# A planned attention and mixing kernel: batch 0's q without its zeros, one pair of scores a unit earlier, last stores in halves

## The chip, the core and the metric

The kernel runs on one core of a Trainium2 chip. The time is the device time of one execution in microseconds (us). The kernel before takes 584.44 us, the median of 3 runs (584.28 to 584.83). The core has a matrix engine (TensorE: PE in the profile, with its weight loads as PEld), a vector engine (VectorE: DVE), a scalar engine (ScalarE: ACT), GpSimd (POOL), and SyncE (SP), whose queue issues every DMA here. Each engine executes its own instructions in a fixed order; semaphores make one engine wait for another. The trace shows the profiled execution, one more run, of 583.05 us.

## The reference, cut to what matters

There are 8 batches, 8 heads, 576 positions and head size 64. The first four heads see a window of the last 32 positions, the other four a window of 128 positions of which every fourth counts.

```python
scores = (1.0 / np.sqrt(D)) * np.matmul(q, k.transpose(0, 1, 3, 2))
scores = np.where(masks[None, :, :, :], scores, -1000000000.0)
scores = scores - np.max(scores, axis=-1, keepdims=True)
attn = np.exp(scores)
attn = attn / (np.sum(attn, axis=-1, keepdims=True) + 1e-09)
x = np.matmul(attn, v)                      # heads side by side: (8, 576, 512)
theta = x @ w_theta
zr, zi = x * np.cos(theta), x * np.sin(theta)
y = np.einsum('ts,bsd->btd', w_tok_r, zr) + np.einsum('ts,bsd->btd', w_tok_i, zi)
u = x + y
out = u + np.maximum(u @ w_ch, 0.0)
```

## The kernel before, in words

**Attention by pairs.** A batch's 8 heads are 4 pairs; each pair takes 128 partitions, one head in the lower 64 and the other in the upper 64. On the host, q is laid out block-diagonally: `qT` holds, for each block of 32 queries, 32 columns for the first head and 32 for the second, and where one head has its values the other has zeros. So one matmul with 128 rows gives the scores of both heads against their window of 64 keys (L468), and half of the bytes of q are zeros: 576 KB per pair, of which 288 KB are values. The four pairs of batch 0 have their own places for q (`q0_0` to `q0_3`, in buffers that later stage weights).

Batch 0's mask is added on PE by matmuls with `idb` (L424). Then DVE takes the row maximum (`mx`, L430) and subtracts it (`P`, L433) in two halves of 5 and 4 blocks, ACT takes the exponential (L493), DVE sums it (`sm`, L495) and makes the reciprocal (L507, L508), POOL multiplies (L510), PE turns the result over (`pT`, L561), DVE and ACT bring it back (`pt`, L536, L539), PE multiplies by v (`o`, L617), and ACT copies the attention output out (`x`, L581). In later batches DVE adds the mask and takes the maximum in one instruction per block (L409), ACT's exponential (L504) works block by block, and DVE turns P over by 32x32 transposes (`pt`, L525).

**Weights.** The three weight matrices arrive as 64-bit integers that hold the reference's doubles' bits. `unpack` makes floats with extra bits of them in place, with steps on DVE (L332, L337, L342) and ACT (L334, L340); `split` then makes a high and a low part (ACT L350, POOL L352). `st_wth` is the staging of `w_theta` (4 pieces), `st_wtk` of the token matrix (5 early pieces for the first half of the positions, 5 late ones for the second), `st_wch` of the channel matrix (4 pieces).

**Mixing.** For each of five position tiles, theta is x times `w_theta` (L667 for batch 0, L685 later), and the trig chain makes sine and cosine of it (ACT L787, DVE L789, ACT L796, L698, L705), multiplies by x (DVE L750 or L748) and splits the result (`zh`, `zl`: ACT L644 or DVE L641, POOL L646). Then come 16 units of PE work per batch: 8 token units (4 channel blocks for each half of the positions, 27 matmuls each, L850, added to x by DVE L825 and split again into `u` by ACT L828 and POOL L830) and 8 channel units (12 matmuls each, L880, finished by DVE L859).

**What sets the order.** Batch 0 and the attention, theta and trig of batch 1 are written by a planner (`Order`). Each task is a generator that names an engine and an assumed duration, or an event that it needs; a task has a rank; whenever an engine comes free in the planner's own clock, the ready task of the lowest rank takes it. The order found is pinned. An assumed DMA takes its bytes at a fixed rate, so the order of the first part of the program depends on how many bytes the planner sees ahead of each weight. From batch 1 on, `phase(b, b + 1)` writes the 16 units of batch b with the attention and theta of batch b+1 between them; `S_AT`, `PV_AT`, `TURN_AT` say at which unit a pair's scores, value product and turning are written. Numbers 2 and 3 there are the last two pairs of batch b+1, and 4 and 5 the first two pairs of batch b+2. PE keeps that order; the other engines are ordered by a scheduler.

**The end.** After the second half of an output block is done, `finish` stores the block of 128 x 576 values (L865).

Of the kernel before, what the change touches and what calls it, by code (L numbers as in the profile page):

```python
# [8 lines left out]
F32 = mybir.dt.float32  # L9
F32R = mybir.dt.float32r  # L10
BF16 = mybir.dt.bfloat16
# [6 lines left out]
B, H, S, D = 8, 8, 576, 64  # L18
DM = H * D
NP = H // 2  # L20
QB = 32
BW = 2 * QB
NJ = S // (2 * QB)
# [20 lines left out]

S_AT = {2: 0, 3: 1, 4: 4, 5: 6}
PV_AT = {0: 0, 1: 1, 2: 2, 3: 4}
TURN_AT = {2: 0, 3: 1, 4: 5}
TURN_TH = {5: 1}  # L50
# [11 lines left out]
class Order:  # L62
# [13 lines left out]
    def pin(self, ins):  # L76
        if self.live:
            self.tc.keep_in_program_order(ins)

    def signal(self, event):  # L80
        self.events[event] = self.now

    def go(self, gen, rank=None):
        if not self.live:
            for _ in gen:
                pass
            return
        self.serial += 1
        t = [self.rank if rank is None else rank, self.serial, self.now, gen, None, 0.0]
        self.tasks.append(t)  # L90
        self.advance(t)
# [39 lines left out]
def dve(n):  # L131
    return 67 + 1.04 * n
# [6 lines left out]
def act(n):  # L139
    return 95 + 0.83 * n  # L140


def pool(n):
    return 2.36 * n


def dma(n):
    return 128 * 4 * n / 360.0


@with_exitstack
def build(ctx, tc, qT, kT, vw, wth, wtk, wch, maskb, ident, identb, outT):
    nc = tc.nc
    cp = ctx.enter_context(tc.tile_pool(name="const", bufs=1))
    ap = ctx.enter_context(tc.tile_pool(name="attn", bufs=2))
# [12 lines left out]
    pin, go, signal = od.pin, od.go, od.signal  # L168
# [20 lines left out]
    def take(tag, bufs, n=None):  # L189
        n = reserve(tag) if n is None else n  # L190
        if od.live:
            if n >= bufs:
                yield None, ("free", tag, n - bufs)
            if n:
                yield None, ("got", tag, n - 1)
            signal(("got", tag, n))
        return n

    def give(tag, n):
        if od.live:  # L200
            signal(("free", tag, n))
# [9 lines left out]
    qks, vs = {}, {}  # L211
# [15 lines left out]
    def load_va(n):  # L227
        if n >= B * NP:
            return
        b, pr = divmod(n, NP)  # L230
        r = yield from take("va", 2)
        va = ap.tile([128, VA, 128], F32, tag="va", name=f"va{b}_{pr}")
        yield "DMA", dma(VA * 128)
        pin(nc.sync.dma_start(va, vw[b, pr, :, :VA]))
        vs["a", b, pr] = (va, r)
        signal(("va", b, pr))

    def load_vb(n):
        if n >= B * NP:
            return  # L240
        b, pr = divmod(n, NP)
        if n == NP - 1:
            r = None
            vb = hp.tile([128, DM], F32R, tag="zl8", name="first_vb").bitcast(F32)
            vb = vb.rearrange("p (a b) -> p a b", b=128)
        else:
            r = yield from take("vb", 1)
            vb = ap.tile([128, NJ - VA, 128], F32, tag="vb", name=f"vb{b}_{pr}", bufs=1)
        yield "DMA", dma((NJ - VA) * 128)
        pin(nc.sync.dma_start(vb, vw[b, pr, :, VA:]))  # L250
        vs["b", b, pr] = (vb, r)
        signal(("vb", b, pr))
# [12 lines left out]
    mskb = cp.tile([128, 6, BW], BF16, name="mskb")  # L265
    idb = cp.tile([128, 128], BF16, name="idb")
    halfpi = cp.tile([128, 1], F32, name="halfpi")
    pqs, pts = [], []

    def first_loads():  # L270
        yield "DMA", dma(3 * BW + 64)
        pin(nc.sync.dma_start(mskb, maskb.bitcast(BF16)))
        pin(nc.sync.dma_start(idb, identb.bitcast(BF16)))
        for pr in range(NP):
            yield from take(f"xh{pr}", 1, 0)
            yield from take(f"u{pr}", 1, 0)
            pqs.append(hp.tile([128, 2, S], F32R, tag=f"xh{pr}", name=f"P0_{pr}").bitcast(F32)[:, 0])
            q = hp.tile([128, 2, S], F32R, tag=f"u{pr}", name=f"q0_{pr}").bitcast(F32)
            q = q.rearrange("p a b -> p (a b)").rearrange("p (a b) -> p a b", b=2 * QB)
            k = first_k[:, KE * pr:KE * pr + KE]  # L280
            yield "DMA", dma(2 * S)
            pin(nc.sync.dma_start(q, qT[0, pr]))
            yield "DMA", dma(KE)
            pin(nc.sync.dma_start(k, kT[0, pr]))
            qks[0, pr] = (q, k, None)
            if pr == 0:
                yield "DMA", dma(128)
                pin(nc.sync.dma_start(idt, ident))
            signal(("qk", 0, pr))
        for pr in range(NP // 2):  # L290
            v = first_v[:, NJ * 128 * pr:NJ * 128 * pr + NJ * 128].rearrange("p (a b) -> p a b", b=128)
            yield "DMA", dma(NJ * 128)
            pin(nc.sync.dma_start(v, vw[0, pr]))
            for h, t in (("a", v[:, :VA]), ("b", v[:, VA:])):
                vs[h, 0, pr] = (t, None)
                signal(("v" + h, 0, pr))
        for pr in range(NP // 2, NP):
            yield from load_va(pr)
            yield from load_vb(pr)
# [555 lines left out]
    def finish(b, e, g, ps, rel):  # L855
        ts = slice(HS * g, HS * g + HS)
        x = xf[b, e]
        yield "DVE", dve(HS)
        pin(nc.vector.scalar_tensor_tensor(out=x[:, ts], in0=ps, scalar=0.0, in1=x[:, ts],  # L859
                                           op0=ALU.max, op1=ALU.add))  # L860
        give(*rel)
        signal(("out", b, e, g))
        if g == 1:
            yield "DMA", dma(S)
            pin(nc.sync.dma_start(outT[b, e], x))  # L865

# [20 lines left out]
    def phase(b, nb):  # L887
# [5 lines left out]
        while n <= TH_AT:  # L893
            for p in S_AT:
                if S_AT[p] == n and nb + p // NP < B:
                    go(scores(nb + p // NP, p % NP))
# [56 lines left out]
    UH = {d: reserve(f"u{d}") for d in range(NC)}  # L953
    od.live = True
    go(first_loads(), 0)
    go(consts(), 0)
    for p in range(NP):
# [29 lines left out]
        phase(b, b + 1)  # L987


_INS = ["qT", "kT", "vw", "wth", "wtk", "wch", "maskb", "ident", "identb"]  # L990


def _arrays(inp):
    import numpy as np
    q, k, v = inp["q"], inp["k"], inp["v"]

    def perm(a):
        a = np.array(a, dtype=a.dtype)
        dil = a[:, H // 2:].reshape(B, H // 2, S // 4, 4, D).transpose(0, 1, 3, 2, 4)
        a[:, H // 2:] = dil.reshape(B, H // 2, S, D)  # L1000
        return a

    q, k, v = perm(q), perm(k), perm(v)
    qT = np.zeros((B, NP, 2, D, 2 * NJ, 2, QB), q.dtype)
    qh = q.reshape(B, NP, 2, 2 * NJ, QB, D).transpose(0, 1, 2, 5, 3, 4)
    for hh in range(2):
        qT[:, :, hh, :, :, hh] = qh[:, :, hh]
    qT = qT.reshape(B, NP, 128, 2 * NJ, 2 * QB)
    kT = np.zeros((B, NP, 128, S + 32), k.dtype)
    kT[..., 32:] = k.transpose(0, 1, 3, 2).reshape(B, NP, 128, S)  # L1010
    vp = np.zeros((B, H, S + 32, D), v.dtype)
    vp[:, :, 32:] = v
    vp = vp.reshape(B, NP, 2, S + 32, D).transpose(0, 1, 3, 2, 4).reshape(B, NP, S + 32, 128)
    vw = np.stack([np.concatenate([vp[:, :, BW * j + QB * e:BW * j + QB * e + BW] for e in range(2)], axis=2)
                   for j in range(NJ)], axis=3)
    wth = inp["moe_w_theta"].reshape(NC, 128, DM).transpose(1, 0, 2)
    wch = inp["moe_w_ch"].reshape(NC, 128, DM).transpose(1, 0, 2)
    wr, wi = inp["moe_w_tok_r"].T, inp["moe_w_tok_i"].T
    wtk = np.stack([wr[128 * c:128 * c + 128] for c in range(4)] +
                   [wi[128 * c:128 * c + 128] for c in range(4)] +  # L1020
                   [np.concatenate([wr[512:], wi[512:]], axis=0)], axis=1)
    m = np.zeros((6, 4, QB, BW), bool)
    for n, (j, bound) in enumerate(((1, 0), (0, 0), (2, 144), (4, 288), (6, 432), (7, 432))):
        for quad in range(4):
            qb = 2 * j + quad // 2
            p = QB * qb + np.arange(QB)[:, None]
            c = QB * qb - QB + np.arange(BW)[None, :]
            m[n, quad] = (p - c >= 0) & (p - c < 32) & (c >= 0) & ((p >= bound) == (c >= bound))

    maskb = np.where(m.transpose(1, 2, 0, 3).reshape(128, 6, BW), 0, 0xD000).astype(np.uint16)  # L1030
    wth, wtk, wch = (np.ascontiguousarray(w).view(np.int64) for w in (wth, wtk, wch))
    ident = np.eye(128, dtype=np.float32)
    identb = np.where(ident > 0, 0x3F80, 0).astype(np.uint16)
    return dict(qT=qT, kT=kT, vw=vw, wth=wth, wtk=wtk, wch=wch, maskb=maskb, ident=ident, identb=identb)


# [20 lines left out]
```

## Time and profile before

| | us |
|---|---|
| median of 3 runs | 584.44 |
| the profiled execution | 583.05 |
| its span, first to last instruction | 581.3 |
| PE busy in the span | 553.6 (95%) |
| DVE busy | 378.0 (65%) |
| ACT busy | 344.3 (59%) |
| POOL busy | 222.6 (38%) |
| first matmul of scores | at 6.8 |
| early token unit's last input of batch 0 done | at 66.4 |
| start of batch 1's token units | at 143.8 |
| last instruction of the last output on DVE | 577.9 to 578.3 |

The part of the profile that counts here is in three stages: a start in which PE has little to do (to about 66 us), a long middle in which PE is nearly always busy, and a tail after the last matmul. The prediction shows the lines of each.

### The profile page before, as it was taken

How to read it: one execution, taken by the hardware profiler on the slowest of the kernel's cores; microseconds unless marked ns; L12 is line 12 of the kernel's file. 1: busy time of each engine (PE TensorE's matmuls, PEld its weight loads, DVE VectorE, ACT ScalarE, POOL GpSimd, SP SyncE). 2: the span in 40 equal slices, each digit the busy share in tenths (PEclk: the TensorE clock that was granted, in tenths of full speed). 3: DMA queues.
4: the chain of work that ended last, by engine and by line, in shares of the span. 5: the costliest groups of instructions: out<-in, count | busy, mean ns of one | idle time of the engine just before them, and what ended most of it. 6: DMA issues, size and time to landing. Idle time of an engine off the chain costs nothing.

```text
span 581.3 us, 13989 instructions
## 1 busy us (share of the span) xinstructions
PE 553.6 (95%) x5464; PEld 502.7 (86%) x5464; DVE 378.0 (65%) x1156; ACT 344.3 (59%) x939; POOL 222.6 (38%) x206
## 2 busy tenths in 40 slices
PE   5997898999999999999999999999999999999997
PEld 4743787989999899989999899988999899989997
DVE  3879798865666668756765768766775767545112
ACT  1498967767553884459554784349555685266110
POOL 2228855625133352316224262225323263326120
PEclk9999699899999999999999999999999999999999
DMA  8991437502648054551747145560746223321002
GB/s 298 399 367 42 145 110 259 192 0 87 204 144 220 6 191 146 162 162 49 240 146 179 47 151 180 139 191 4 252 143 172 90 83 101 71 94 62 22 0 82
DMA packets 45010, 81.91 MB, mean 141 GB/s; under 512 B 3856, under 2 KB 17936, under 8 KB 44944
## 3 DMA queue, kind: packets, MB, share of 16 engines
q1 hardware_dynamic: 44944, 81.02, 43.6%
q8 instruction: 43, 0.70, 0.5%
q14 instruction: 23, 0.19, 0.1%
HBM read 64.49 MB, written 16.52 MB: 139 GB/s over the span
## 4 chain that ended last, share of the span: by engine, by line
DVE 32%; PE 29%; ACT 26%; POOL 6%; issue 4%; DMA 2%; SPq 1%; ACTq 0%; DVEq 0%; POOLq 0%
DVE pt L525 14%; PE y L850 13%; ACT P L504 10%; PE c L880 7%; PE th L685 4%; DVE P L409 4%; POOL zl L646 3%; DVE xh L599 2%; POOL P L510 2%; ACT zh L644 2%; PE s L468 2%; ACT K L698 2%; ACT K L787 2%; ACT cos L705 2%; ACT th L796 2%
## 5 line engine op out<-in xcount | busy, mean ns | idle before, releaser
L830 POOL TENSOR_TENSOR u<-x,u 128x288 fp32r<-128x288 f32 x64 | 54.8, 857 | 189.2 <-ACT u L828 189.2
L525 DVE STREAM_TRANSPOSE pt<-P 32x288 f32<-32x288 f32 x224 | 104.9, 468 | 12.5 <-POOL P L510 8.9
L880 PE MATMUL c<-u,late_wc 128*128 128x288 f32 x768 | 108.9, 295 | 0.0
L880 PEld LDWEIGHTS c<-u,late_wc 128*128 128x128 f32 x768 | 105.9, 188 | 2.8
L850 PE MATMUL y<-wtkh,zh 128*128 128x288 f32 x288 | 90.1, 313 | 1.1 <-ACT zh L644 1.1
L850 PE MATMUL y<-wtkh,zl 128*128 128x288 f32 x288 | 86.2, 299 | 4.0 <-POOL zl L646 4.0
L828 ACT CAST u<-x 128x288 fp32r<-128x288 f32 x64 | 27.4, 430 | 104.0 <-DVE x L825 104.0
L646 POOL TENSOR_TENSOR zl<-g,zh 128x512 fp32r<-128x512 f32 x40 | 52.6, 1317 | 94.8 <-ACT zh L644 81.9
L850 PE MATMUL y<-wtkl,zh 128*128 128x288 f32 x288 | 86.0, 298 | 0.0
L685 PE MATMUL th<-wthh,xh 128*128 128x512 f32 x224 | 75.0, 396 | 5.4 <-DVE g L748 5.2
L504 ACT ACTIVATE P<-P,mx 128x64 f32<-128x64 f32 x216 | 72.1, 335 | 13.1 <-DVE mx L498 12.4
L850 PE MATMUL y<-late_wt_b,zh 128*128 128x288 f32 x320 | 68.1, 297 | 0.0
L825 DVE TENSOR_TENSOR x<-y,x 128x288 f32<-128x288 f32 x64 | 28.6, 448 | 54.4 <-PE y L850 54.2
L850 PEld LDWEIGHTS y<-wtkh,zl 128*128 128x128 f32 x288 | 55.1, 191 | 4.7 <-POOL zl L646 4.7
L850 PEld LDWEIGHTS y<-wtkh,zh 128*128 128x128 f32 x288 | 55.0, 191 | 4.8 <-ACT zh L644 2.3
L850 PE MATMUL y<-late_wt_a,zh 128*128 128x288 f32 x256 | 57.4, 305 | 0.0
L850 PEld LDWEIGHTS y<-wtkl,zh 128*128 128x128 f32 x288 | 55.1, 191 | 0.3 <-issue 0.3
L685 PEld LDWEIGHTS th<-wthh,xh 128*128 128x128 f32 x224 | 42.0, 188 | 15.2 <-PE c L880 4.8
L510 POOL TENSOR_TENSOR P<-P,sm 128x576 f32<-128x576 f32 x32 | 37.5, 1173 | 40.7 <-DVE sm L508 17.7
L850 PEld LDWEIGHTS y<-late_wt_b,zh 128*128 128x128 f32 x320 | 51.4, 189 | 0.3
L850 PE MATMUL y<-late_wt_b,zl 128*128 128x288 f32 x160 | 47.3, 296 | 0.0
L581 ACT COPY x<-o 128x576 f32<-128x576 f32 x32 | 29.6, 924 | 28.7 <-PE o L617 23.9
(108 smaller groups left out, 1106.1 us busy)
## 6 DMA issues: line engine op xcount, KB each, us to landing
q<-in_qT_dram SPq DMA_DIRECT2D x32, 576.0 KB, 5.0
va<-in_vw_dram SPq DMA_DIRECT2D x30, 320.0 KB, 3.2
out_dram<-x SPq DMA_DIRECT2D x32, 288.0 KB, 2.1
k<-in_kT_dram SPq DMA_DIRECT2D x28, 304.0 KB, 5.2
vb<-in_vw_dram SPq DMA_DIRECT2D x29, 256.0 KB, 3.7
xd<-xq SPq DMA_DIRECT2D x24, 288.0 KB, 4.8
xn<-xd SPq DMA_DIRECT2D x24, 256.0 KB, 4.9
st_wtk<-in_wtk_dram SPq DMA_DIRECT2D x8, 576.0 KB, 8.8
```

Source lines behind the costliest of these rows:

```text
L409: pin(nc.vector.tensor_tensor_reduce(out=P[:, n], in0=ps[:, n - g0], in1=mskb[:, mask_of(pr, n)], op0=ALU.add, op1=ALU.max, scale=1.0, sca ...
L504: table(nc.scalar.activation(P[:, n], P[:, n], AF.Exp, bias=mx[:, n:n + 1], scale=SCALE, accum_out=sm[:, n:n + 1]))
L510: pin(nc.gpsimd.tensor_tensor(P, P, sm.unsqueeze(2).to_broadcast([128, NJ, BW]), op=ALU.mult))
L525: pin(nc.vector.transpose(pmats[b, pr][k0:k0 + QB, :, hh, QB * e:QB * e + QB], P[p0:p0 + QB, :, QB * o:QB * o + QB]))
L581: pin(nc.scalar.copy(dst, src))
L646: pin(nc.gpsimd.tensor_tensor(lo, z, hi.bitcast(F32), op=ALU.subtract))
L685: pe(nc.tensor.matmul(pt, l, r, start=(n == 0), stop=(n == 3 * NC - 1)))
L825: pin(nc.vector.tensor_tensor(x[:, ts], ps, x[:, ts], op=ALU.add))
L828: pin(nc.scalar.copy(uh[b, d][:, ts], x[:, ts]))
L830: pin(nc.gpsimd.tensor_tensor(ul[b, d][:, ts], x[:, ts], uh[b, d][:, ts].bitcast(F32), op=ALU.subtract))
L850: pe(nc.tensor.matmul(ps, l[:, cs], r, start=(n == 0), stop=(n == 3 * NK - 1)))
L880: pe(nc.tensor.matmul(ps, l[:, cs], r[:, ts], start=(n == 0), stop=(n == 3 * NC - 1)))
```

## The change: what it does

Three edits.

- Batch 0's q is loaded without the zeros. A new input `q0` holds the 288 KB of values per pair; they land in `q_raw` (the buffer of a tile that batch 2 uses first). `q_zero` writes the zeros of each half with two VectorE memsets per pair (64 partitions x 576 elements each), and `q_place` copies the values to their places: the lower half on ScalarE, the upper half on VectorE for pair 0 and on GpSimd for pairs 1 to 3. `mskb` and `idb` are issued behind the first q. The planner sees the new tasks, and half of q's bytes.
- `S_AT` gives the scores of pair "4" (the first pair of batch b+2) with token unit 3 in place of 4, in the five phases that have such a pair.
- The last batch's outputs are stored as two halves of 128 x 288, each as soon as it is done.

```diff
-S_AT = {2: 0, 3: 1, 4: 4, 5: 6}
+S_AT = {2: 0, 3: 1, 4: 3, 5: 6}
...
+    q_raw = cp.tile([128, 5 * DM], F32, tag="xn", name="q_raw")[:, :NP * S]
+    q_raw = q_raw.rearrange("p (n a b) -> p n a b", n=NP, b=QB)
+
+    def q_zero(pr, q, hh):
+
+        yield "DVE", 670
+        pin(nc.vector.memset(q[64 * hh:64 * hh + 64, :, QB - QB * hh:2 * QB - QB * hh], 0.0))
+        signal(("qz", pr, hh))
+
+    def q_place(pr, q, hh):
+        to, src = q[64 * hh:64 * hh + 64, :, QB * hh:QB * hh + QB], q_raw[64 * hh:64 * hh + 64, pr]
+        if hh == 0:
+            yield "ACT", act(S)
+            pin(nc.scalar.copy(to, src))
+        elif pr == 0:
+            yield "DVE", dve(S)
+            pin(nc.vector.tensor_copy(to, src))
+        else:
+            yield "POOL", pool(S)
+            pin(nc.gpsimd.tensor_copy(to, src))
+        signal(("qp", pr, hh))
+
+    def q_ready(pr, q, k):
+        for hh in range(2):
+            yield None, ("qz", pr, hh)
+            yield None, ("qp", pr, hh)
+        yield None, ("k0", pr)
+        qks[0, pr] = (q, k, None)
+        signal(("qk", 0, pr))
+
     def first_loads():
-        yield "DMA", dma(3 * BW + 64)
-        pin(nc.sync.dma_start(mskb, maskb.bitcast(BF16)))
-        pin(nc.sync.dma_start(idb, identb.bitcast(BF16)))
         for pr in range(NP):
...
-            yield "DMA", dma(2 * S)
-            pin(nc.sync.dma_start(q, qT[0, pr]))
+            for hh in range(2):
+                go(q_zero(pr, q, hh), -1)
+            yield "DMA", dma(S)
+            pin(nc.sync.dma_start(q_raw[:, pr], q0[pr]))
+            for hh in range(2):
+                go(q_place(pr, q, hh), 0)
+            if pr == 0:
+                yield "DMA", dma(3 * BW + 64)
+                pin(nc.sync.dma_start(mskb, maskb.bitcast(BF16)))
+                pin(nc.sync.dma_start(idb, identb.bitcast(BF16)))
...
-        if g == 1:
+        if b == B - 1:
+            pin(nc.sync.dma_start(outT[b, e][:, ts], x[:, ts]))
+        elif g == 1:
             yield "DMA", dma(S)
             pin(nc.sync.dma_start(outT[b, e], x))
...
+    q0 = np.ascontiguousarray(qh[0].reshape(NP, 128, 2 * NJ, QB))
```

The planner gives the first part of the program another order on every engine. Three places of it follow; lines behind the new functions stand 35 or more higher in the changed kernel (L430 is L465 there).

DVE, the start of the program, before (`mx`, `P` and `sm` are row maximum, scores and sum; `s_1_0` is pair 1's first half of scores):

```order
L303 MEMSET halfpi 128x1
L430 TENSOR_REDUCE mx_0_116<-s_0_0_118 128x5
L433 TENSOR_TENSOR P_0_104<-s_0_0_118,mx_0_116 128x320
L430 TENSOR_REDUCE mx_0_116<-s_0_5_135 128x4
L433 TENSOR_TENSOR P_0_104<-s_0_5_135,mx_0_116 128x256
L430 TENSOR_REDUCE mx_1_147<-s_1_0_151 128x5
L495 TENSOR_REDUCE sm_0_117<-P_0_104 128x9
L433 TENSOR_TENSOR P_1_114<-s_1_0_151,mx_1_147 128x320
```

And in the change:

```order
L276 MEMSET q_0_98 64x18x32 x2
L338 MEMSET halfpi 128x1
L286 COPY q_0_98<-q_raw 64x18x32
L276 MEMSET q_1_117 64x18x32 x2
L465 TENSOR_REDUCE mx_0_121<-s_0_0_123 128x5
L276 MEMSET q_2_127 64x18x32 x2
L468 TENSOR_TENSOR P_0_97<-s_0_0_123,mx_0_121 128x320
L276 MEMSET q_3_146 64x18x32 x2
L465 TENSOR_REDUCE mx_0_121<-s_0_5_142 128x4
L465 TENSOR_REDUCE mx_1_159<-s_1_0_169 128x5
L468 TENSOR_TENSOR P_0_97<-s_0_5_142,mx_0_121 128x256
L468 TENSOR_TENSOR P_1_116<-s_1_0_169,mx_1_159 128x320
```

Four memsets now stand between the steps of pair 0's first softmax, and the second half of pair 0 stands behind pair 1's first maximum.

DVE again, around the scores of pair 3 in batch 0, before (`st_wth` is the staging of the theta weights):

```order
L430 TENSOR_REDUCE mx_3_226<-s_3_5_302 128x4
L433 TENSOR_TENSOR P_3_154<-s_3_5_302,mx_3_226 128x256
L332 TENSOR_SCALAR st_wth_96<-st_wth_96 128x512
L495 TENSOR_REDUCE sm_3_227<-P_3_154 128x9
L536 COPY pt_107<-pT_2_0_355 64x10x32
L536 COPY pt_107<-pT_2_5_389 64x8x32
L337 TENSOR_SCALAR st_wth_96<-st_wth_96 128x512
L507 TENSOR_SCALAR sm_3_227<-sm_3_227 128x9
```

And in the change:

```order
L465 TENSOR_REDUCE mx_3_250<-s_3_5_326 128x4
L468 TENSOR_TENSOR P_3_145<-s_3_5_326,mx_3_250 128x256
L367 TENSOR_SCALAR st_wth_101<-st_wth_101 128x512
L571 COPY pt_112<-pT_2_0_378 64x10x32
L377 SCALAR_TENSOR_TENSOR st_wth_100<-st_wth_100 128x512
L571 COPY pt_112<-pT_2_5_415 64x8x32
L372 TENSOR_SCALAR st_wth_101<-st_wth_101 128x512
L367 TENSOR_SCALAR st_wth_102<-st_wth_102 128x512
L377 SCALAR_TENSOR_TENSOR st_wth_101<-st_wth_101 128x512
L530 TENSOR_REDUCE sm_3_251<-P_3_145 128x9
L367 TENSOR_SCALAR st_wtk_0_161<-st_wtk_0_161 128x576
L377 SCALAR_TENSOR_TENSOR st_wth_102<-st_wth_102 128x512
```

Where one step of the first theta piece stood between pair 3's subtraction and its sum, there now stand seven rows, five of them steps of theta pieces 1 to 3; the first theta piece is done before pair 3's maximum.

DVE in phase 1, around the first masked maximum of pair "4" (`P_0_2099` before, `P_0_2084` in the change); `pt_109` before and `pt_114` in the change is pair 3's turned P, and each L409 row (L444 in the change) is followed by one that reads its maximum. Before:

```order
L729 STREAM_TRANSPOSE xq_1884<-x_2_2037 128x18x32
L525 STREAM_TRANSPOSE pt_109<-P_3_1886 32x9x32 x8
L597 TENSOR_TENSOR xh_2_2062<-x_2_2037,xh_2_2062 128x64
L599 TENSOR_TENSOR xh_2_2062<-x_2_2037,xh_2_2062 128x512
L825 TENSOR_TENSOR x_3_1340<-y_3_0_2067,x_3_1340 128x288
L409 ISA P_0_2099,mx_0_2100<-s_0_0_2102,mskb 128x64
L409 ISA mx_0_2100 128x1
```

And in the change:

```order
L764 STREAM_TRANSPOSE xq_1901<-x_2_2054 128x18x32
L444 ISA P_0_2084,mx_0_2085<-s_0_0_2087,mskb 128x64
L444 ISA mx_0_2085 128x1
L560 STREAM_TRANSPOSE pt_114<-P_3_1903 32x9x32 x8
L632 TENSOR_TENSOR xh_2_2079<-x_2_2054,xh_2_2079 128x64
L634 TENSOR_TENSOR xh_2_2079<-x_2_2054,xh_2_2079 128x512
L444 ISA P_0_2084,mx_0_2085<-s_0_0_2087,mskb 128x64
L444 ISA mx_0_2085 128x1
```

One of the nine masked maxima moves ahead of the eight transposes; the other eight stay behind L599, and L825 of `y_3_0` moves from ahead of them to behind them, still ahead of the step (L498) that hands the maxima to ACT.

More of the change, by code (lines that the diff above doesn't have):

```diff
@@ L151, in build @@
 @with_exitstack
-def build(ctx, tc, qT, kT, vw, wth, wtk, wch, maskb, ident, identb, outT):
+def build(ctx, tc, qT, q0, kT, vw, wth, wtk, wch, maskb, ident, identb, outT):
     nc = tc.nc
@@ L280, in first_loads @@
             k = first_k[:, KE * pr:KE * pr + KE]
-            yield "DMA", dma(2 * S)
-            pin(nc.sync.dma_start(q, qT[0, pr]))
+            for hh in range(2):
[8 more added lines that the diff above has]
+                pin(nc.sync.dma_start(idb, identb.bitcast(BF16)))
             yield "DMA", dma(KE)
             pin(nc.sync.dma_start(k, kT[0, pr]))
-            qks[0, pr] = (q, k, None)
+            go(q_ready(pr, q, k), 0)
             if pr == 0:
@@ L288, in first_loads @@
                 pin(nc.sync.dma_start(idt, ident))
-            signal(("qk", 0, pr))
+            signal(("k0", pr))
         for pr in range(NP // 2):
@@ L987, in build @@
         phase(b, b + 1)
-_INS = ["qT", "kT", "vw", "wth", "wtk", "wch", "maskb", "ident", "identb"]
+_INS = ["qT", "q0", "kT", "vw", "wth", "wtk", "wch", "maskb", "ident", "identb"]
 def _arrays(inp):
@@ L1033, in _arrays @@
     identb = np.where(ident > 0, 0x3F80, 0).astype(np.uint16)
-    return dict(qT=qT, kT=kT, vw=vw, wth=wth, wtk=wtk, wch=wch, maskb=maskb, ident=ident, identb=identb)
+    return dict(qT=qT, q0=q0, kT=kT, vw=vw, wth=wth, wtk=wtk, wch=wch, maskb=maskb, ident=ident, identb=identb)
 def kernel(**inputs):
```

## The prediction, as put on record

> **What bounds the kernel now.** I read the busy table by stages first, then the waits of PE, then the chain and the timeline at the places that the change touches. The table gives, for each stretch in us, the length and the busy us of each engine (PE, PEld, DVE, ACT, POOL), the granted clock, the share of time in which the DMA engines were busy, and what they moved.
>
> ```profile
> 6.80:30.00 23.20, 21.45 (x420) 17.27 (x422) 16.81 (x40) 8.93 (x16) 4.87 (x4) 1.00 1.03 395
> 30.00:66.40 36.40, 29.76 (x194) 16.22 (x188) 32.77 (x83) 33.05 (x68) 22.53 (x17) 0.91 0.58 211
> 66.40:76.00 9.60, 9.53 (x70) 9.30 (x72) 7.08 (x17) 9.38 (x32) 8.99 (x8) 0.82 0.00 0
> 76.00:106.00 30.00, 27.00 (x371) 23.91 (x367) 25.79 (x61) 20.13 (x76) 13.74 (x14) 0.94 0.67 221
> 106.00:143.80 37.80, 36.62 (x292) 32.94 (x288) 26.58 (x57) 28.66 (x60) 19.06 (x17) 1.00 0.18 65
> 210.00:276.00 66.00, 64.99 (x654) 60.64 (x654) 45.10 (x158) 40.65 (x121) 24.09 (x24) 1.00 0.47 144
> ```
>
> From 30 to 66.4 DVE and ACT are busy for 32.8 and 33.1 of 36.4 us: that stage ends when they have got through their work. From 6.8 to 30 DVE is busy for only 16.8 of 23.2 us, 6.4 us idle. From 66.4 on PE is the bound; in a whole batch (210 to 276) it idles 1.0 us of 66. So a us won before 66.4 is a us at the end, unless a wait behind it eats it.
>
> ```profile
> PE th L685 <- DVE g L748: 5.2, 5, 1.2
> PE s L424 <- ACT P L485: 3.0, 2, 2.0
> PE s L468 <- DMA first_k<-in_kT_dram: 3.2, 1, 3.2
> 64.85 1.58 POOL zl L646
> 66.47 8.67 PE y L850 x52
> ```
>
> The waits of PE (total, times, longest) and two pieces of the chain: the one regular wait of the batches is 5.2 us in five places, theta behind the trig chain; and the start ends where the last `zl` lets the token units run.
>
> **The loads.** In the timeline the four first issues, in the chain the piece that PE waits for, then the bandwidth in three stretches:
>
> ```profile
> 0.74 0.38 SPq L272 DMA_DIRECT2D mskb<-in_maskb_dram  x1
> 1.64 0.42 SPq L282 DMA_DIRECT2D q<-in_qT_dram  x1
> 2.11 0.43 SPq L284 DMA_DIRECT2D first_k<-in_kT_dram  x1
> 2.11 4.56 DMA first_k<-in_kT_dram
> 3.00:4.00 1.00, 0.45 (x2) 0.13 (x2) 0.00 (x0) 0.00 (x0) 0.00 (x0) 1.00 0.66 194
> 5.00:6.00 1.00, 0.00 (x0) 0.00 (x0) 0.00 (x0) 0.00 (x0) 0.00 (x0) 1.00 1.07 345
> 36.00:40.00 4.00, 4.00 (x12) 1.69 (x13) 3.05 (x6) 3.98 (x7) 2.32 (x2) 1.00 1.06 396
> ```
>
> k of pair 0 lands at 2.11 + 4.56 = 6.67, as the fourth issue behind 96 + 32 + 576 KB. In the change it is the fourth again, behind 288 + 96 + 32 KB: 288 KB less, 0.85 us at 345 GB/s. The large transfer is now issued at 0.74 in place of 1.64, so the engines no longer run at 194 GB/s on small ones until 4; I add 0.35 for that. Scores begin **1.2 us earlier** (0.7 by bytes alone at 400 GB/s; 1.8 if k lands as soon as the fixed part of a small load allows), at 5.6.
>
> The copies lie beside that:
>
> ```profile
> 20.33 0.64 ACT L581 COPY x<-o 128x576 f32<-128x576 f32 x1
> 13.34 1.15 POOL L510 TENSOR_TENSOR P<-P,sm 128x576 f32<-128x576 f32 x1 [10.56 <-DVE sm L508]
> 10.48 0.68 ACT L493 ACTIVATE P<-P 128x576 f32<-128x576 f32 x1 [8.47 <-DVE P L433]
> ```
>
> The first q lands at about 4 (issued at 0.74, a small load's 2.0 us and 0.85 us of bytes, with room), ACT's copy takes 0.64, DVE's no more: done at 4.8, ahead of k. POOL's three copies take 0.6 to 1.5 each; it has nothing to do before 13.3, and q of pair 3, behind some 2250 KB, lands near 10, ahead of ACT's first exponential. If that cover went (q of pair 3 later than 12), ACT's exponential of pair 0 would wait behind its copy, one for one. All copies: 0.
>
> In all 1152 KB less are loaded at the start. At 396 GB/s that is 3.0 us by which every weight lands earlier; the engines take it up only where they idle.
>
> **The memsets.** Their order rows show two ahead of the first copy and two of pair 1 before the scores: hidden, DVE does nothing before 8.18. Four, those of pairs 2 and 3, stand between the maximum and the subtraction of pair 0 and behind it. There is no such memset in the trace. Nearest rows:
>
> ```profile
> 33.39 0.44 DVE L332 TENSOR_SCALAR st_wtk<-st_wtk 128x576 f32<-128x576 f32 x1
> 11.72 0.74 DVE L495 TENSOR_REDUCE sm<-P 128x9 f32<-128x576 f32 x1
> 8.18 0.49 DVE L430 TENSOR_REDUCE mx<-s 128x5 f32<-128x320 f32 x1 [7.32 <-PE s L468]
> ```
>
> 576 elements take 0.44 at the fast rate for one source and 0.74 in a reduction at the slow one; I take the middle, 0.6. Four are **+2.4 us** of DVE work (1.8 to 3.0). The Trainium skill (VectorE: DVE Perf Modes, Zero memsets can be issued as uint32) says that a memset takes one cycle for each element at any dtype, which at the page's 0.96 GHz is an estimate of 0.6 us and speaks against the fast row; by that row alone the sum would come out 0.6 us lower.
>
> What queues behind them: the scores now end at 7.0, so the maximum is at 7.5, the subtraction behind two memsets at 8.7 to 9.2 (9.19 before), and the second half, behind two more and behind pair 1's maximum, at about 12.2 (10.45 before). ACT's first exponential, at 10.48 now, comes near 12.2.
>
> **What DVE gains.** DVE's idle time before 30 and its reasons:
>
> ```profile
> DVE mx L430 <- PE s L468: 9.3, 4, 7.3
> DVE st_wth L342 <- ACT st_wth L340: 2.1, 2, 1.3
> DVE pt L536 <- PE pT L561: 1.3, 3, 0.7
> 26.57 1.71 DVE L332 TENSOR_SCALAR st_wth<-st_wth 128x512 f32<-128x512 f32 x2
> ```
>
> Without the 7.3 us before the first scores, there are 2.0 for later scores, 2.1 for ACT's unpacking, 1.3 for the turned P. In the change the memsets fill the first gaps, and steps of theta pieces 0 to 3 stand where DVE waited for pair 3. Placing the rows of the new order one behind another with these durations, I am left with waits for scores of 0.45 and 0.65, for exponentials of 0.35, for turned P of 1.2: 2.7 us in place of 6.4. So **-3.7 us** (bounds: 0, if each wait only moves; -6.4, if all go). From 30 to 64 DVE's idle time (36.40 - 32.77 = 3.6) is kept, since trig has the same chain of ACT and DVE.
>
> Two more terms. DVE ends this stage with the product of K by x of tile 3, on which ACT's last `zh` and POOL's last `zl` wait. In the new order five late unpacking steps stand ahead of it, in place of three, and only five of pair 1's nine masked maxima.
>
> ```profile
> 55.54 0.93 DVE L332 TENSOR_SCALAR st_wtk<-st_wtk 128x576 f32<-128x576 f32 x1
> 45.35 0.21 DVE L409 CUSTOM_DVE_ANT_0 P<-s,mskb 128x64 f32<-128x64 f32 x1
> 46.07 0.68 DVE L750 TENSOR_TENSOR K<-xn,K 128x512 f32<-128x512 f32 x1
> 63.38 0.68 DVE L750 TENSOR_TENSOR K<-xn,K 128x512 f32<-128x512 f32 x1
> ```
>
> One step of 576 columns and one of 288: 0.93 + 0.47 = **+1.4**; four maxima, five of which fill 45.35 to 46.07, so 0.145 each: **-0.6**. Sum for the start: -1.2 + 2.4 - 3.7 + 1.4 - 0.6 = **-1.7 us**. The last `zl` then ends near 64.7.
>
> **The moved scores.** PE does the same work. Whether the regular wait shrinks depends on when ACT gets pair 4's maxima:
>
> ```profile
> 229.26 3.83 DVE L525 STREAM_TRANSPOSE pt<-P 32x288 f32<-32x288 f32 x8
> 233.86 0.45 DVE L825 TENSOR_TENSOR x<-y,x 128x288 f32<-128x288 f32 x1
> 234.23 0.21 DVE L409 CUSTOM_DVE_ANT_0 P<-s,mskb 128x64 f32<-128x64 f32 x1
> 235.91 0.35 ACT L504 ACTIVATE P<-P,mx 128x64 f32<-128x64 f32 x1 [1.13 <-DVE mx L498]
> ```
>
> DVE works without a gap from the transposes at 229.26 to the hand-over at 235.9; the maxima wait for DVE, not for their scores, done at 230.9. In the new order one maximum goes ahead of the transposes and L825 behind the maxima, but still ahead of the hand-over: the same rows in another order, so ACT starts when it did. **0** (bounds: the 0.45 of L825 either way, in each of five phases). Pair 4's PSUM banks and P buffer are free by 222.4, its q and k are asked for a whole unit before, so PE takes no new wait.
>
> **The halves.** Issues on SP at the end find its queue empty. Sizes and time to landing:
>
> ```profile
> out_dram<-x SPq DMA_DIRECT2D x32, 288.0 KB, 2.1
> mskb<-in_maskb_dram SPq DMA_DIRECT2D x1, 96.0 KB, 2.0
> idb<-in_identb_dram SPq DMA_DIRECT2D x1, 32.0 KB, 1.9
> ```
>
> 0.2 us for 256 KB, so 144 KB less on the last store is **-0.1** (at most 0.4 at 396 GB/s). The Trainium skill (DMA: Bandwidth & Descriptors, Anatomy of one DMA) fits 2.0 us and bytes / 436e3 to GpSimd's path, an estimate of 0.34 us less for the half; its 2.7 us for a whole store is not what these rows show, so the measured 2.1 decides, and by the page the sum would be 0.2 lower.
>
> **Sum.** -1.7 + 0 - 0.1 = -1.8 us. The profiled execution, 583.05 (1.75 around its span of 581.3), would be 581.25; it lay 1.4 below the median, so the median goes from 584.44 to **582.6**.
>
> **The rivals.**
>
> *The waits only move (slower).* The four memsets push pair 0's softmax back, and each later score, exponential and turned P is as late; DVE idles its 6.4 us all the same. For it: every step of pairs 0 to 2 comes 1 to 1.6 us later in my placing, and pair 3's sum 6 us later. Against it: DVE has other work listed there. It decides where DVE's idle time from the first scores to 30 stays over 4.5 us. -1.8 + 3.7 = +1.9: 586.3.
>
> *The gain is lost behind the start (no change).* From 76 to 106 PE idles 3 us, behind exponentials of batch 1 and the late weights:
>
> ```profile
> 88.27 4.89 DMA st_wch<-in_wch_dram
> 101.18 0.30 PE L424 MATMUL s<-mskb,idb 128*128 128x64 bf16 x2 [1.96 <-ACT P L485]
> ```
>
> These chains are made of ACT and DVE work that is not shorter; if PE comes to them 1.7 us sooner it waits 1.7 us more. Against it: the same engines start them sooner. -0.1: 584.3.
>
> *The loads were the bound (much faster).* If the 3.0 us of DMA show in full and DVE loses all 6.4 us of idle time: -1.8 - 2.7 = -4.5, 579.9. Against it: the first theta piece is touched at 23 only, three us behind its landing.
>
> *The moved scores pay.* If L825's 0.45 leaves the chain, five times: -2.2 more, 580.4.
>
> **How the numbers follow.** What a measurement can tell is 0.2%, 1.17 us: 583.27 and 585.61. The forecast gets 0.44 (its own range 581.3 to 583.9), the slower rival 0.17, the lost gain 0.19, the loads 0.14, the scores 0.06. Faster: 0.40 of the forecast's, both fast rivals: 0.60. Same: 0.04 and 0.19, 0.23. Slower: 0.17. The range leaves out the far half of the slower and of the loads rival: 579.9 to 585.8.
>
> **What would show it.** Right: the first scores near 5.6, memsets of 0.6, the first exponential near 12, DVE idle below 3.5 us to 30, the last early `zl` ending between 64 and 65.5, the five theta waits still 1 us each, the same shift at the first unit of batch 1 (143.8 now) as at the `zl`, the last landing 0.1 sooner. Wrong: memsets of 0.3 (0.6 to 1.2 us more gain), scores that do not start earlier, a batch that no longer takes 66.3 us, or a shift at 66 that is gone at 143.

## The result, and the profile after

The changed kernel takes **592.44 us** (median of 4 runs, 592.39 to 593.42) against 584.36 us (median of 4, 584.03 to 584.83) for the kernel before: 1.0144 times as long, with a 95% interval of 1.013 to 1.0159. That is 8 us slower where 1.8 us faster was forecast, and outside the predicted range. The profiled execution took 592.41 us, its span is 590.6 (581.3 before).

The busy table by stages of the changed kernel, with the columns as before (length, busy us of PE, PEld, DVE, ACT, POOL, granted clock, DMA share, GB/s):

```profile
6.80:30.00 23.20, 20.47 (x358) 15.47 (x357) 19.52 (x45) 11.51 (x21) 5.45 (x6) 1.00 1.02 389
30.00:66.40 36.40, 29.38 (x235) 16.26 (x229) 31.64 (x73) 30.14 (x50) 21.03 (x16) 0.91 0.44 157
66.40:76.00 9.60, 8.79 (x73) 8.26 (x69) 5.28 (x21) 9.60 (x42) 7.79 (x8) 1.00 0.27 94
76.00:106.00 30.00, 25.01 (x353) 21.77 (x353) 28.12 (x61) 21.50 (x79) 14.89 (x13) 1.00 0.62 198
106.00:143.80 37.80, 34.19 (x241) 30.41 (x242) 27.44 (x50) 24.03 (x53) 15.08 (x14) 0.95 0.19 67
143.80:210.00 66.20, 63.68 (x636) 58.85 (x635) 43.38 (x154) 39.17 (x117) 22.17 (x22) 0.97 0.48 141
210.00:276.00 66.00, 64.50 (x656) 60.42 (x655) 44.39 (x157) 39.30 (x118) 22.75 (x22) 1.00 0.49 146
```

DVE is busier up to 30 (idle 3.7 us in place of 6.4), as was meant, but less busy from 30 to 66.4 (idle 4.8 in place of 3.6): the work was done earlier, and then something else was missing. The timeline shows what. First the rows that answer to the prediction's list, then those of pair 3 and of the trig chain:

```profile
5.80 1.34 PE L503 MATMUL s<-first_k,q 128*64 128x64 f32 x20 [1.15 <-DMA first_k<-in_kT_dram]
7.73 0.54 DVE L276 MEMSET q<- 64x576 f32 x1
8.42 0.54 DVE L276 MEMSET q<- 64x576 f32 x1 [0.16 <-issue]
12.16 0.68 ACT L528 ACTIVATE P<-P 128x576 f32<-128x576 f32 x1 [0.71 <-DVE P L468]
...
28.11 0.69 ACT L528 ACTIVATE P<-P 128x576 f32<-128x576 f32 x1
41.60 1.19 ACT L616 COPY x<-o 128x576 f32<-128x576 f32 x1
44.29 0.59 ACT L822 ACTIVATE K<-th 64x512 int32<-64x512 f32 x1
65.53 0.69 DVE L785 TENSOR_TENSOR K<-xn,K 128x512 f32<-128x512 f32 x1
67.53 1.27 POOL L681 TENSOR_TENSOR zl<-K,zh 128x512 fp32r<-128x512 f32 x1 [0.82 <-ACT zh L679]
```

The same three of the kernel before (pair 3's exponential, pair 3's x, the first step of the trig chain):

```profile
23.15 0.68 ACT L493 ACTIVATE P<-P 128x576 f32<-128x576 f32 x1 [0.71 <-DVE P L433]
34.67 1.23 ACT L581 COPY x<-o 128x576 f32<-128x576 f32 x1
37.47 0.62 ACT L787 ACTIVATE K<-th 64x512 int32<-64x512 f32 x1
```

Pair 3's exponential comes 5.0 us later, its x 6.9, the trig chain 6.8. The last early `zl` ends at 67.53 + 1.27 = 68.8, against 66.4: the start lost 2.4 us where 1.7 were to be won.

The larger part of the loss lies behind it. In each run the first token matmul of a batch can be read off (us from the span's start):

| | first of batch 0 | 1 | 2 | 3 | 5 | 7 | last of all |
|---|---|---|---|---|---|---|---|
| before | 49.6 | 143.7 | 210.0 | 276.2 | 409.0 | 536.3 | 564.8 |
| changed | 55.6 | 150.0 | 219.2 | 285.7 | 418.3 | 545.8 | 574.3 |
| later by | 6.0 | 6.3 | 9.2 | 9.5 | 9.3 | 9.5 | 9.5 |

So only 0.3 us more is lost behind batch 2's start. PE's own waits between 70 and 220 us, in the timeline of the changed kernel and then of the one before (where the wait of 1.96 at 101.18, shown in the prediction, belongs to them):

```profile
84.14 0.31 PE L459 MATMUL s<-mskb,idb 128*128 128x64 bf16 x5 [2.57 <-ACT P L520]
90.76 0.40 PE L885 MATMUL y<-late_wt_b,zh 128*128 128x288 f32 x1 [0.97 <-POOL late_wt_b L387]
99.19 0.69 PE L652 MATMUL o<-pt,vb 128*64 128x64 f32 x16 [0.58 <-DMA vb<-in_vw_dram]
104.53 0.30 PE L459 MATMUL s<-mskb,idb 128*128 128x64 bf16 x2 [0.88 <-ACT P L520]
110.04 0.69 PE L652 MATMUL o<-pt,vb 128*64 128x64 f32 x16 [1.04 <-DMA vb<-in_vw_dram]
120.79 3.25 PE L917 MATMUL c<-u,late_wc 128*128 128x288 f32 x12 [2.38 <-DVE x L860]
153.14 0.41 PE L885 MATMUL y<-wtkh,zl 128*128 128x288 f32 x1 [0.21 <-POOL zl L681]
202.87 0.77 PE L720 MATMUL th<-wthh,xh 128*128 128x512 f32 x1 [2.31 <-DVE g L783]
```

```profile
82.14 0.31 PE L424 MATMUL s<-mskb,idb 128*128 128x64 bf16 x5 [1.04 <-ACT P L485]
119.78 0.50 PE L685 MATMUL th<-wthh,xh 128*128 128x512 f32 x1 [0.17 <-DVE g L784]
124.61 0.63 PE L759 MATMUL xn<-idt,x 128*128 128x128 f32 x4 [1.01 <-DVE g L750]
195.10 0.47 PE L685 MATMUL th<-wthh,xh 128*128 128x512 f32 x1 [0.95 <-DVE g L748]
```

The eight sum to 10.9 us, the five of before to 5.1: 5.8 more. Two of the waits have slow matmuls behind them (twelve of `c` take 3.25 us, 1.74 before). The granted clock is at half for 3.4 us there. Each pair of rows has the 3.4 us ahead of the slow stretch and then the stretch itself:

```profile
117.41:120.82 3.41, 0.92 (x6) 0.48 (x5) 3.38 (x6) 1.31 (x3) 2.41 (x3) 1.00 0.00 0
120.82:124.23 3.41, 3.41 (x13) 3.25 (x14) 3.25 (x8) 0.39 (x1) 2.31 (x3) 0.50 0.00 0
199.33:202.74 3.41, 1.23 (x10) 0.99 (x8) 2.36 (x4) 3.29 (x6) 0.00 (x0) 1.00 0.00 0
202.74:206.15 3.41, 3.29 (x8) 2.64 (x9) 1.82 (x3) 3.38 (x7) 1.00 (x1) 0.50 0.02 5
```

Behind 66.4 the kernel before has two such stretches as well, one at the end of the start and one behind its wait at 101.18:

```profile
67.58:70.99 3.41, 3.41 (x16) 3.41 (x15) 2.06 (x7) 3.41 (x17) 2.80 (x4) 0.50 0.00 0
101.71:105.12 3.41, 3.41 (x30) 3.03 (x29) 2.40 (x8) 2.19 (x10) 1.25 (x1) 0.50 0.92 315
```

Each costs up to half of its length, 1.7 us, but there are two in both executions, and the mean granted clock of both is 0.988: the clock explains none of the difference. The balance of the span: +2.4 at the start, +5.8 of waits, +0.3 from batch 2 on, 8.5 of 9.3; 0.8 is not attributed.

### The profile page after: what moved, and what is told of

Same layout as the page of the kernel before. It is cut to its first block, busy times and chain, and to the rows that moved or that the text cites. A ratio compares the mean times of both kernels' runs of the same rounds, so it can differ in the third digit from the quotient of the medians.

```text
span 590.6 us, 14019 instructions
## 1 busy us (share of the span) xinstructions
PE 554.5 (94%) x5464; PEld 502.7 (85%) x5464; DVE 386.7 (65%) x1165; ACT 347.5 (59%) x943; POOL 222.0 (38%) x209
## 4 chain that ended last, share of the span: by engine, by line
DVE 33%; PE 30%; ACT 24%; POOL 5%; issue 4%; DMA 2%; SPq 0%; ACTq 0%; DVEq 0%; POOLq 0%
DVE pt L560 15%; PE y L885 10%; ACT P L539 10%; PE c L917 9%; PE th L720 6%; DVE P L444 4%; DVE xh L634 2%; POOL P L545 2%; POOL zl L681 2%; ACT zh L679 2%; DMA st_wch<-in_wch_dram 2%; PE s L503 2%; ACT K L822 2%; ACT K L733 1%; ACT L831 1%
## 5 line engine op out<-in xcount | busy, mean ns | idle before, releaser
L917 PE MATMUL c<-u,late_wc 128*128 128x288 f32 x768 | 111.0, 298 | 2.6 <-DVE x L860 2.4
L917 PEld LDWEIGHTS c<-u,late_wc 128*128 128x128 f32 x768 | 107.2, 190 | 6.0 <-DVE x L860 2.9
L860 DVE TENSOR_TENSOR x<-y,x 128x288 f32<-128x288 f32 x64 | 28.6, 449 | 53.5 <-PE y L885 53.2
```

Of the source, the lines that this page charges most:

```text
L860: pin(nc.vector.tensor_tensor(x[:, ts], ps, x[:, ts], op=ALU.add))
L917: pe(nc.tensor.matmul(ps, l[:, cs], r[:, ts], start=(n == 0), stop=(n == 3 * NC - 1)))
```

## Experiments

Two theories at first. A: the planner's new order makes the loss. B: the moved scores make much of it (the first theta wait is 2.3 us, all five 8.1). A third, C: the memsets, copies and earlier weights collide with other work. Every ratio is to the kernel before on the same chip, and can differ a little from the quotient of the two medians.

**The edits apart.** `s_only` is the kernel before with `S_AT = {..., 4: 3, ...}`, `h_only` with the stores in halves, `q_only` with the q edit and its planner.

> The kernel before with S_AT alone changed (pair "4" with token unit 3). Theory A (the planner's new order of the first part makes the 8 us; the moved scores do nothing): 584.4 us within 0.5, the five theta waits 5.2 us in all as before. Theory B (the moved scores cost: in the changed kernel the theta wait of phase 1 is 2.3 us in place of 1.0, with slow matmuls behind it, and the five waits are 8.1 us in all): 586.5 to 588 us, the theta waits about 8 us.

Measured: 1.0015 (1.0 to 1.003), 584.23 us against 583.15. Neither: the waits grew to 7.3 us, but more than half of the growth is PE coming earlier: counted from a batch's first token matmul, theta goes on at 51.6 us here and at 51.4 before. So four of the five batches last 66.5 us in place of 66.3, some 0.2 us a phase, which agrees with the ratio (whose interval reaches 1.0). Part of it shows at pair 4's hand-over to ACT. DVE's and ACT's rows there of the run:

```profile
235.38 0.17 DVE L498 TENSOR_SCALAR mx<-mx 128x9 f32<-128x9 f32 x1
235.49 0.43 ACT L828 CAST u<-x 128x288 fp32r<-128x288 f32 x1 [6.68 <-DVE x L825]
235.83 0.34 ACT L504 ACTIVATE P<-P,mx 128x64 f32<-128x64 f32 x1
```

The kernel before has its L498 there at 235.64 and the exponential 0.27 later (235.91, shown in the prediction). Here it is 0.45 later, because L825 now ends just ahead of L498, and ACT first casts what L825 made: 0.18 us. But L498 itself comes 0.1 sooner in its batch, so this exponential is less than 0.1 late; the next pair's is 0.2 late, and what adds the rest there is not shown.

> The kernel before with the last batch's stores in halves alone. Every theory: 584.2 us (0.1 less, at most 0.4 less), the last landing after the last instruction of DVE some 0.1 us sooner than before.

Measured: 0.9993 (0.9979 to 1.0007): not to be told from no change. The stores of 144 KB land in 1.8 us, those of 288 KB in 2.1 to 2.4 (medians of each run).

> The kernel before with the q edit alone, planner and all (S_AT and the stores as before). Theory A: 592 us, nearly all of the loss, and the waits of PE between 80 and 121 us as in the changed kernel (exponential 2.6, late_wt_b 1.0, vb 1.6, x of the token unit 2.4). Theory B: 589 to 590 us, with the phase 1 theta wait back at 1.0 us.

Measured: 1.0113 (1.0092 to 1.0133), 590.89 us; repeated later, 1.0115 (1.0095 to 1.0135). Nearly all of the loss, and PE's waits at the named places are those of the changed kernel, but for that on `late_wt_b`, which is not there. From 76 to 222 us they are 9.7 us in all, against 5.1 before. The theta wait of phase 1 is 1.7 us, between A's and B's. A holds so far.

**The q edit with the order of before.** The planner gets the times of before; `q_zero` and `q_place` have no `yield` here, so it doesn't see the memsets and copies (against the kernel before, cut):

```diff
+            qz.append(q)
+            if pr < 2:
+                q_zero(q)
+        yield "DMA", dma(3 * BW + 64)
+        for pr in range(NP):
...
             yield "DMA", dma(2 * S)
-            pin(nc.sync.dma_start(q, qT[0, pr]))
+            pin(nc.sync.dma_start(q_raw[:, pr], q0[pr]))
...
+            q_place(pr, q)
+            if pr == 0:
+                q_zero(qz[2])
+                q_zero(qz[3])
```

> The q edit with the order of before: the planner is given the times of before for the loads and does not see memsets and copies, so every engine keeps its order of before; four memsets stand ahead of the first copy and four behind it, all ahead of the first maximum; each copy on the engine of the change. Theory A: the loss is gone, 582.0 to 584.0 us, first scores at 5.8 and the first maximum at 7.2 as in the changed kernel, no memset between steps of the softmax. Rival C (the early weights, memsets and copies themselves collide with other work, whatever the order): 588 us or more.

Measured: **0.9979** (0.9963 to 0.9994), medians 582.71 us against 583.15. The loss is gone, as A has it; in the trace every engine has its rows in the order of before, but for the memsets and copies. The edit itself is a small gain at best: 1.2 us by the ratio, 0.4 by the medians. Every memset is out of the way before the first maximum, and the last `zl` ends at 65.6, 0.8 sooner than in the trace of before (rows of DVE and POOL):

```profile
6.42 0.54 DVE L275 MEMSET q<- 64x576 f32 x1 [0.16 <-issue]
7.20 0.49 DVE L452 TENSOR_REDUCE mx<-s 128x5 f32<-128x320 f32 x1 [0.24 <-PE s L490]
63.99 1.57 POOL L668 TENSOR_TENSOR zl<-K,zh 128x512 fp32r<-128x512 f32 x1 [0.61 <-ACT zh L666]
```

That 0.8 is no proof of the gain, though. `h_only` has the start of before, with its first scores at 7.16, and its last `zl` ends at 65.6 too:

```profile
63.99 1.56 POOL L646 TENSOR_TENSOR zl<-K,zh 128x512 fp32r<-128x512 f32 x1 [0.62 <-ACT zh L644]
```

One and the same start differs by as much from one execution to the next, so what makes the gain is not shown.

**The reverse.** `new_order_old_work` keeps the planner's tasks as times (`yield "DVE", 670` and so on) but writes no memset and no copy, and loads the whole q.

> The reverse of the run with the order of before: every engine has the order that the q edit gives, but the loads are those of before (576 KB a pair, no zeros written, no copies). Theory A (the order alone makes the loss): 588.5 to 592 us, ratio to before 1.008 to 1.014, first scores back at 6.8, first trig step near 44. Rival C (memsets, copies and early loads carry part of it): at most 586 us, ratio below 1.004.

Measured: 1.0146 (1.0121 to 1.0171), 591.66 us against 583.56. With none of the change's work, and every engine's rows in the order of `q_only`, the loss is all there, just above A's ratio: that the order makes the loss is shown from both sides, and C falls. The trig chain starts as late as in the changed kernel (timeline of ACT):

```profile
41.73 1.19 ACT L609 COPY x<-o 128x576 f32<-128x576 f32 x1
44.12 0.59 ACT L815 ACTIVATE K<-th 64x512 int32<-64x512 f32 x1 [0.91 <-PE th L695]
```

**The memsets' price.** `zeros_inline` is `q_same_order` with the four memsets moved to where the change has them.

```diff
         pin(nc.vector.tensor_reduce(mx[:, g0:g1], ps, op=ALU.max, ...))
+        inline = key == ("mask", 0, 0, 0)
+        if inline:
+            q_zero(qz[2])
...
+            if inline:
+                q_zero(qz[3])
```

> The run with the order of before, but with the four memsets of pairs 2 and 3 between pair 0's maximum and subtraction and behind it, as the change has them; nothing else is moved. If DVE's work bounds the start, as the prediction had it: four times 0.7 us (0.54 and a gap of 0.16), less the 0.4 that DVE waits there, +2.4 us against that run: ratio to before 1.002, last early zl 2.4 us later (near 68). If the start has slack behind pair 0: ratio 0.998, the last early zl within 0.5 us of 65.6.

Measured: 1.0025 (1.0011 to 1.004). Against `q_same_order` that is 0.46%, 2.7 us, and the last `zl` ends 2.6 us later:

```profile
66.57 1.56 POOL L671 TENSOR_TENSOR zl<-K,zh 128x512 fp32r<-128x512 f32 x1 [0.62 <-ACT zh L669]
```

DVE's chain there has next to no slack: the four memsets are 2.8 us from start to start, and nearly all of it is paid.

**What in the order?** Theory D: with half of q's bytes the weights land earlier in the planner's clock, and since `theta_unpack` (rank 1.54) outranks pair 3 (1.72 to 1.76), its steps pass pair 3. `q_rank` is `q_only` with one number changed:

```diff
-... theta_unpack=1.54, ...
+... theta_unpack=1.8, ...
```

> The q edit with its planner, but the rank of the theta weights' unpacking 1.8 in place of 1.54, so that it no longer goes ahead of pair 3 (ranks 1.72 to 1.76). Theory D (the weights land 3 us earlier, pass pair 3's softmax on DVE and ACT, and the trig chain starts late): first trig step of ACT near 38 in place of 44, last early zl near 65, and most of the loss gone, ratio at most 1.004. Rival E (the loss is in the order behind the start: late loads of v behind the channel weights on SP, POOL's order, the channel unit ahead of theta): ratio 1.008 or more although the trig starts early.

Measured: 1.0091 (1.007 to 1.0111). D is right about the start and wrong about the loss. The trig chain begins at 38.67 and the last `zl` ends at 66.9 (timeline), yet batch 1 begins at 150.2, 6.5 us later than before. PE's waits now have other names (total, times, longest):

```profile
38.67 0.57 ACT L822 ACTIVATE K<-th 64x512 int32<-64x512 f32 x1
65.61 1.27 POOL L681 TENSOR_TENSOR zl<-K,zh 128x512 fp32r<-128x512 f32 x1 [0.53 <-ACT zh L679]
```

```profile
PE s L459 <- DVE st_wtk L377: 2.2, 1, 2.2
PE s L459 <- ACT P L520: 2.1, 1, 2.1
PE c L915 <- DVE x L894: 1.9, 1, 1.9
```

So in this order, a third one, the start is repaired and most of the loss stays: it lies behind the start (E), and not in one fixed wait. In this execution up to 3.4 us of it are the clock's: between 66.4 and the start of batch 1 it has four stretches at half clock, from 67.5, 84.5, 105.0 and 125.5, where before has two.

**One wait.** In the changed kernel the addition that frees a bank for the second channel unit (L860) stands on DVE behind two steps of `xh`. `q_evac` is `q_only` with that one row moved ahead of them; the other four engines keep their order. `q_only_again` is its partner.

> The q edit alone once more, as the partner of the next run on the same chip: ratio to before 1.0113 as measured, 1.009 to 1.013.

> The q edit with one row moved: on DVE the addition of the last token unit of batch 0 (L860, which frees the PSUM bank of the second channel unit) stands ahead of the two steps of xh of pair 2 in place of behind them; every other engine's order is as before the move. If the 2.4 us wait of PE for it is a real loss and the slow matmuls behind it (3.1 us for twelve in place of 1.7) come from the wait: 2 to 3.5 us less than its partner (ratio to it 0.994 to 0.997), the twelve matmuls at 1.7 us. If PE only waits for the next thing there (the split of x of pair 3 on POOL, done near 123.5): within 0.5 us of its partner.

Measured: 1.0089 (1.0068 to 1.0111) against 1.0115 of its partner; medians 588.5 and 590.72, so some 1.5 to 2.2 us less, but the two intervals overlap. The traces, partner first:

```profile
121.75 3.25 PE L915 MATMUL c<-u,late_wc 128*128 128x288 f32 x12 [2.38 <-DVE x L860]
```

```profile
118.46 1.85 PE L919 MATMUL c<-u,late_wc 128*128 128x288 f32 x12 [0.19 <-DVE x L862]
125.78 0.50 PE L722 MATMUL th<-wthh,xh 128*128 128x512 f32 x1 [0.65 <-DVE g L821]
130.62 0.63 PE L796 MATMUL xn<-idt,x 128*128 128x128 f32 x4 [1.05 <-DVE g L787]
```

At the place itself 2.38 - 0.19, 2.2 us of wait, are won, and two new waits of 1.7 us take most of it back. The slow clock can't be counted as won with the wait: in the first `q_only` run, whose order is the partner's, the same wait stood there, and the twelve matmuls took 1.85:

```profile
120.50 1.85 PE L915 MATMUL c<-u,late_wc 128*128 128x288 f32 x12 [2.38 <-DVE x L860]
```

Batch 1 begins at 148.6 there, at 150.9 in the partner and at 148.4 in `q_evac`. So the wait was real, the slow matmuls need not come from it, and whether the move gains anything is not shown.

**Is any other order as good?** Three runs do exactly the work of before and only tell the planner something else: `plan_rate` assumes 372 in place of 360 bytes/ns for DMAs, `plan_bytes` half of q's bytes, `plan_tasks` the memsets and copies as times.

> The kernel before, its work unchanged; only the planner's assumed DMA rate is 372 in place of 360 bytes/ns, and it finds another order (DVE's order of the first softmaxes and the theta weights stays as before, later pieces change on all engines). Theory H (the ranks were chosen for the costs of before, and nearly any other order of the planner is worse, mostly behind the start): 586 to 590 us, ratio 1.004 or more. Rival I (the planner is robust, and only the change's passing of pair 3 by the weights is bad): ratio within 0.998 to 1.002.

> The kernel before, its work unchanged; the planner is told half of q's bytes, but sees no memsets and copies. Of the two things that the planner is told in the change: if the bytes bring the loss (weights thought to be there earlier go ahead of pair 3), 588 to 592 us; if the memsets and copies bring it, within 0.3% of before.

> The kernel before, its work unchanged; the planner sees the memsets and copies (as times, with no instruction) but all of q's bytes. The counterpart of the run on the bytes: if the bytes bring the loss, within 0.3% of before; if any change of the planner's input does (theory H), 1.004 or more here too.

Measured: 1.0032 (1.0016 to 1.0048), 1.0041 (1.0028 to 1.0055), 1.0047 (1.0027 to 1.0067). All three are slower. `plan_tasks` reaches H's ratio, `plan_rate` lies between H and I, and `plan_bytes` fits neither of its two cases. The change's two inputs together gave 1.0146, more than both apart: which of the two makes the loss stays open. With 3% on one assumed rate the planner loses 1.9 us. First token matmul of batches 0, 1 and 2: 48.6, 146.3, 212.6 for `plan_rate` (49.6, 143.7, 210.0 before), so it too loses between batch 0's and batch 1's units.

**Candidates.** `change_same_order` is all three edits on `q_same_order`; `pool_copies` is `q_same_order` with all copies of pairs 1 to 3 on POOL, and the halves.

> All three edits, with the order of before kept at the start (the run with the order of before, and S_AT and the halves). If the parts add: 0.9979 times 1.0015 times 0.9993, 0.9987 of before, 582.5 to 583.5 us on a chip where before takes 583.5. If the theta waits of the moved scores grow on the earlier start: 1.001.

> A candidate: the order of before, all copies of pairs 1 to 3 on POOL (ACT's first exponential no longer waits 0.5 us behind a copy), stores of the last batch in halves. Expected 0.9965 to 0.998 of before: the 0.8 us of the earlier start and about 0.1 to 0.4 from the halves. If the 0.5 us of ACT counts, 0.996; if the start is given back behind it, 0.999.

Measured: 0.9993 (0.9978 to 1.0007) and 0.9984 (0.9969 to 1.0). The first agrees with the parts' product of 0.9987, the second lies just above the range that was expected. With `q_same_order`'s 0.9979 (0.9963 to 0.9994) all three intervals overlap: none is shown to be the best, and all are over 1% faster than the changed kernel.

## Why the prediction was wrong, step by step

- **Scores earlier, 1.2 us.** They started at 5.80, 1.0 earlier. Right in kind; whether it reaches the end is not shown, since the start of before varies by 0.8 by itself.
- **Copies hidden.** Right. The first exponential came at 12.16 (12.2 predicted).
- **Four memsets, +2.4 (bounds 1.8 to 3.0).** Each takes 0.54 and leaves a gap of 0.16; `zeros_inline` paid 2.7. Right in kind, a little low. The Trainium skill (VectorE: DVE Perf Modes, Zero memsets can be issued as uint32) has one cycle for each element, at its 0.96 GHz an estimate of 0.6 us. That lies between the row's 0.54 and the 0.70 from start to start.
- **DVE's idle time shrinks, -3.7.** This is the step that failed in the start. Idle time did shrink, by 2.7. But I took each us of it as a us off the end, "a us won before 66.4 is a us at the end", because DVE and ACT were the busiest engines of the stage. What filled the gaps was weight work that nobody waited for yet, and it stood in front of pair 3, on whose x theta and then the whole trig chain wait. The chain began 6.8 us later, and the early work could not make up for it: +2.4 in place of -1.7. With the scores' -1.0 and the memsets' +2.7 as measured, the rest of the start came to +0.7, where -3.7 + 1.4 - 0.6 = -2.9 was forecast. The slower rival saw that pair 3 comes "6 us later" and its +1.9 is near the start's +2.4, but that is luck: its mechanism, idle time that only moves, did not happen (3.7 us, where it needed over 4.5).
- **Five late steps and four maxima, +0.8 net.** Not tested apart. The +1.4 rests on a step of 576 columns at 0.93 us (55.54), while the same step stands at 0.44 (33.39) in the rows for the memsets; why the longer one was taken is not said.
- **From 66.4 on a shift is only carried.** This failed most. The new order differs on every engine up to batch 2's start, and I gave that part no term. There the shift grows from 2.4 us to 9.2, 6.8 of the 9.5 at the end, with 5.8 us of added waits of PE. `q_rank` agrees, with the start repaired (+0.5 us for the last `zl`, but 0.91% of the whole). Which rows of the order make these waits is shown for none of them alone.
- **Moved scores, 0 (0.45 either way).** Measured +0.15% (0 to 0.3), some 0.2 us a phase: inside the bounds. One step missed was ACT's cast that L825 releases; DVE's rows alone were followed.
- **Halves, -0.1 (at most 0.4).** 0.9993 (0.9979 to 1.0007), in agreement, and too small to show.
- **The rivals.** None had a planner's order that is worse as such, though its order follows from the ranks, and three other inputs with the work of before all made it worse (by 0.3 to 0.5%). The rival of no change looked at the right place, PE's waits from 76 us on, but let them take back only what the start won.

## What to carry to other kernels

Where a planner or scheduler writes the order, an edit that feeds it other costs is two changes: the work and the order. Measure them apart by holding the order (the edit unseen by the planner) and by holding the work (the planner fed, the edit not written); here they were -0.2% and +1.5%. Idle time of the busiest engine is a gain only if what fills it is on the chain that everything waits for: follow that chain (pair 3, x, theta, trig) and ask what now stands in front of it.

## What the runs showed of the hardware

An idle stretch of PE can cost a second time, but not each time. Behind the waits of 2.38 and 2.31 us in the changed kernel the granted clock was 0.50 for 3.4 us, while behind the same wait of 2.38 in `q_only` it stayed at 1.00, as it did behind 2.57 at 84.14 in the changed kernel. The length of the wait alone does not decide.

What the traces do show is a grid. In each of the 16, up to the last matmul, the half clock comes in stretches of 3.41 us or whole multiples of it, and their starts lie whole multiples of 3.41 us apart (in the changed kernel 59.38, 120.82 and 202.74, 18 and 24 steps). Where the grid lies differs from one execution to the next. In the changed kernel the wait at 120.79 falls into one step, which leaves PE busy for 0.92 of 3.41 us (117.41 in the rows of the result). In `q_only`, which has a slow stretch from 85.24 on and so a step that ends 10 steps later, at 119.37, it is spread over two:

```profile
115.96:119.37 3.41, 2.04 (x12) 1.60 (x12) 3.33 (x6) 2.41 (x4) 3.02 (x3) 1.00 0.00 0
119.37:122.79 3.42, 2.29 (x15) 2.09 (x16) 3.32 (x7) 0.43 (x1) 1.96 (x4) 1.00 0.00 0
```

From 15 us on, in all 16 traces, each step at full clock with PE busy for under 1.6 us was followed by one at half clock, and none with more than 1.9 us was. The Trainium skill (TensorE: Matmul & The Clock Gate, Part 1: The HAM clock gate) has the clock at half after an idle window of about 3.4 us that runs freely, and at full after a busy one. The length of the slow stretches and their grid agree with that. The window ahead of them was not idle throughout here: PE was busy for 0.92 and 1.23 of its 3.41 us.
